# A [1, 576] result accumulated in four column groups of one PSUM bank instead of two groups in two banks

## The chip, the cores and the metric

The kernel runs on one core of one Trainium2 chip. The core has five engines that run side by side and meet through semaphores: TensorE (PE, matrix products), VectorE (DVE), ScalarE (ACT), GpSimd (POOL) and SyncE (SP, here only an issuer of DMAs). Sixteen DMA engines move data between device memory and SBUF, the on-chip memory of 128 partitions. TensorE writes its products into PSUM, which has 128 partitions and eight banks. The metric is the device time of one execution in microseconds; lower is better. The time shown is a median of three runs. A profile is one further execution, and its own time is given beside its span.

A matmul in this kernel computes `lhsT.T @ rhs`: `lhsT` (up to 128 partitions by up to 128 columns) is loaded into the array first, then the columns of `rhs` stream through it. Where `lhsT` has at most 32 columns, only a strip of 32 of the array's columns is needed; the profile calls the loads PEld and the streams PE. `tile_position=(0, 32 * n)` says which of the four strips (column groups 0 to 3) a matmul uses, and its output then lies on the PSUM partitions from 32 n on.

## The reference

One token x of width 576 goes through a layer norm and then through two branches, whose outputs are added to x:

```
xn  = layernorm(x)
A   = attention(xn @ wq, last 4096 keys and values of 16 heads, 32 query heads) @ wo
z   = gelu(xn @ w_in);  z1, z2 = halves of 2304
B   = (z1 * (w_sp * layernorm(z2) + b_sp)) @ w_out
out = x + A + B                          # [1, 1, 576]
```

`wo` is 4096 by 576 and `w_out` 2304 by 576. All inputs and the output are bfloat16. With one token, every product is a vector times a matrix, and almost all of the work is reading: 51 MB of keys, values and weights.

## The kernel before, in words

Everything that is read in bulk goes through one queue, SyncE's, in this order: `wq`, keys of head groups 0 and 1, `w_in`, keys 2, values 0, keys 3, values 1 to 3, `w_out`, `wo`. A head group is four key heads, and there are four groups (index `g`). The buffers are four slots of SBUF (tags a to d) that are reused, so a load waits until its slot was read. `wo` comes in five loads of 14, 9, 6, 2 and 1 "rows" (lines 107 to 109). Such a row is one step of a contraction: 128 partitions by 576 columns. `w_out` has 18 rows (`wout_sb`), `wo` 32 (`wo_sb`).

The order of the instructions on each engine is the order of the program text (the schedule is manual, line 69). For each head group the program turns keys (`keys`, DVE transposes), multiplies them with the queries (`scores`, PE), takes a maximum and an exponential (`sm_a`, DVE and ACT), transposes the probabilities (`sm_b`, DVE and ACT copies, L306), multiplies them with the values (`pv`, L329: eight rounds of four matmuls of 512 columns, one in each column group, into one bank) and normalizes (`tail`: `recip`, `norm`, `y_mms` at L350 and `y_copy` at L357). `y_mms(g)` works in column group g, and `y_copy(g)` puts the 32 values of each partition into `Y`. `Y`, [128, 32], is the attention output, one column for each row of `wo`. The gated branch runs in between: `z_mms` (L365, 162 matmuls with 128 columns of weights and two columns of data), then `z_exp`, `z_gelu` and `z_norm`, which leave `hv`, [128, 18], one column for each row of `w_out`.

The result is accumulated in PSUM in two pieces of 264 and 312 columns (`CUT`), each on one partition: `acc[0]` on partition 0 of one bank, `acc[1]` on partition 32 of another. Line 439 opens both with a product of one and `xrow`, which adds x itself; the first piece reuses the bank from which `zps` has been read. `out_mms` (L465) then adds one row: one column of `hv` or `Y` as weights, 264 columns of data into group 0 and 312 into group 1. All 50 rows are added at the end of the program: after `pv(3)` come the 18 rows of `hv` in three calls of six, with `tail(3)` between the second and the third, then the 32 rows of `Y`, for which the five loads of `wo` are awaited one after the other.

Then the two pieces are copied to `res`, a single row of 576 bfloat16 values: the first by DVE (L480), the second by ACT (L481). ACT issues the store (L482), one run of 1152 bytes.

Around the result the lines are, in the program before:

```python
CUT = (0, 264, D)
        for n in range(2):
            nc.tensor.matmul(acc[n], lhsT=lhs[:, col:col + 1], rhs=wv[:, CUT[n]:CUT[n + 1]],
                             start=False, stop=last, tile_position=(0, 32 * n))
    nc.vector.tensor_copy(res[:, 0:CUT[1]], acc[0])
    nc.scalar.copy(res[:, CUT[1]:D], acc[1])
    nc.scalar.dma_start(out.flatten_outer_dims(), res[:])
```

Of the kernel before, what the change touches and what calls it, by code (L numbers as in the profile page):

```python
# [8 lines left out]
FP32 = mybir.dt.float32  # L9
BF16 = mybir.dt.bfloat16  # L10
# [4 lines left out]
D = 576  # L15
# [10 lines left out]
TC = TP // 2  # L26
NR = 98
NF = FH // 128
CUT = (0, 264, D)
XP = D // 3  # L30
EPS = 1e-5
SCALE = DH ** -0.5
# [5 lines left out]
def kernel(  # L38
# [14 lines left out]
    nc = tc.nc  # L53
    P = nc.NUM_PARTITIONS
# [4 lines left out]
    const = ctx.enter_context(tc.tile_pool(name="const", bufs=1))  # L59
# [4 lines left out]
    ps_o = ctx.enter_context(tc.tile_pool(name="ps_o", bufs=1, space=bass.MemoryType.PSUM))  # L64
    ps_m = ctx.enter_context(tc.tile_pool(name="ps_m", bufs=1, space=bass.MemoryType.PSUM))
    ps_a = ctx.enter_context(tc.tile_pool(name="ps_a", bufs=1, space=bass.MemoryType.PSUM))
    ps_b = ctx.enter_context(tc.tile_pool(name="ps_b", bufs=1, space=bass.MemoryType.PSUM))

    ctx.enter_context(tc.manual_schedule())

# [41 lines left out]
    xrow = const.tile([1, D], BF16, name="xrow")  # L112
# [15 lines left out]
    ones_b = const.tile([1, P], BF16, name="ones_b")  # L128
# [36 lines left out]
    for n in range(2):  # L165
        t = ps_s.tile([P, 2, 512], FP32, name=f"S{n}")
# [15 lines left out]
    for j in range(NS):  # L182
# [8 lines left out]
        out=junk[:], in0=x_col[:], in1=x_col[:], scale=1.0, scalar=0.0,  # L191
# [40 lines left out]
    for k in range(4):  # L232
        for be in range(4):
            nc.tensor.matmul(
                qps2[:, k, be, :].rearrange("p (r g) -> p r g", r=2),
                lhsT=q_rep[0:NR, 2 * k + be // 2, be % 2].rearrange("p a d -> p (a d)"),
                rhs=idq, start=True, stop=True)
# [23 lines left out]
    def scores(g, c):  # L261
        kv = KT.pop((g, c))[:].rearrange("p (t s) b r x e -> p b e x t r s", s=2)
        for be in range(4):
            for x in range(GK):
                nc.tensor.matmul(  # L265
                    S[g % 2][32 * x:32 * x + 8, c, :],
                    lhsT=Qb[:, GK * g + x, be].rearrange("p a h -> p (a h)"),
                    rhs=kv[:, be // 2, be % 2, x],
                    start=(be == 0), stop=(be == 3), tile_position=(0, 32 * x),
                )  # L270
# [161 lines left out]
    zg = z_exp(zps)  # L432
    keys(2, 1)
    scores(2, 1)
    acc = []
    for n, pool in enumerate((ps_a, ps_b)):
        t = pool.tile([P, 512], FP32, name=f"acc{n}", tag="ab"[n])
        acc.append(t[32 * n:32 * n + 1, 0:CUT[n + 1] - CUT[n]])
        nc.tensor.matmul(acc[n], lhsT=ones_b[:, 0:1], rhs=xrow[:, CUT[n]:CUT[n + 1]],
                         start=True, stop=False, tile_position=(0, 32 * n))  # L440
    G, sz = z_gelu(*zg)
    sums(0)
# [18 lines left out]
    pv(3)  # L461

    def out_mms(lhs, col, wv, last):
        for n in range(2):
            nc.tensor.matmul(acc[n], lhsT=lhs[:, col:col + 1], rhs=wv[:, CUT[n]:CUT[n + 1]],  # L465
                             start=False, stop=last, tile_position=(0, 32 * n))

    def out_hv(c):
        for t, wv in wout_sb[6 * c:6 * c + 6]:
            out_mms(hv, t, wv, False)  # L470
# [5 lines left out]
    for t, wv in wo_sb:  # L476
        out_mms(Y, t, wv, t == 31)

    res = const.tile([1, D], BF16, name="res")
    nc.vector.tensor_copy(res[:, 0:CUT[1]], acc[0])  # L480
    nc.scalar.copy(res[:, CUT[1]:D], acc[1])  # L481
    nc.scalar.dma_start(out.flatten_outer_dims(), res[:])  # L482


# [28 lines left out]
```

## Time and profile before

| | |
|---|---|
| median of 3 runs (lowest to highest) | 126.86 us (126.86 to 126.87) |
| profiled execution, its own time | 126.89 us |
| its span, first to last instruction | 125.1 us |
| busy: PE, PEld | 70.8 us (57%), 28.9 us (23%) |
| busy: DVE, ACT, POOL | 78.5 us (63%), 43.2 us (34%), 7.1 us (6%) |
| read from device memory | 50.96 MB, 407 GB/s over the span |
| chain of work that ended last | DMA 61%, DVE 30%, PE 5% |
| mean granted TensorE clock | 0.754 of full speed |

How to read the lines that follow. The page gives the span in 40 equal slices, each digit being a busy share in tenths; PEclk is the TensorE clock that was granted, in tenths of full speed. The chain of waits is followed back from the last instruction and shown in order of time: start, length, what. In the timeline a line is a group of like instructions one after another: start, length, engine, line of the program, operation, tile written <- tiles read, count, and in brackets how long the engine stood idle before and what ended that. In the groups, the numbers behind the bar are busy time in us and the mean length of one in ns, then the idle time before them. "issue" is time in which the engine waited for nothing that the profile shows. Matmuls are pipelined and their ends are modelled; their starts are recorded.

### The profile page before, as it was taken

The page shows a single profiled execution, that of the slowest core. Times are in us where ns is not written, and L with a number is a line of the kernel's source. Part 1 is how long each engine was busy: PE and PEld are TensorE (multiplying, and loading weights), DVE is VectorE, ACT ScalarE, POOL GpSimd, SP SyncE. Part 2 cuts the span into 40 slices and gives each one's busy share as a digit, 9 for nine tenths or more (in the row PEclk, how much of TensorE's full clock was granted, in tenths as well). Part 3 has the DMA queues.
Part 4 walks back from the last instruction along what each step waited for, and adds up shares of the span by engine and source line. Part 5 has one row for each costly group of instructions (what it writes and reads, how often), then busy time and mean ns, then how long its engine had stood idle before and what let it go on. Part 6 is the DMA issues. An engine that isn't in the chain of part 4 may idle for free.

```text
span 125.1 us, 1617 instructions
## 1 busy us (share of the span) xinstructions
PE 70.8 (57%) x626; PEld 28.9 (23%) x626; DVE 78.5 (63%) x150; ACT 43.2 (34%) x101; POOL 7.1 (6%) x19
## 2 busy tenths in 40 slices
PE   0012841009878469998390992059892932049992
PEld 0001201001101013998000131002211411015850
DVE  6745025899799976308999367999938359003301
ACT  2100011000000956996069008707801941940001
POOL 2961000000000000000000000000000100000000
PEclk9999998555995867755559599657998555555899
DMA  4999899998999999898999989999999999999960
GB/s 118 511 422 440 385 471 440 398 492 356 487 420 402 385 493 461 377 492 372 461 451 398 482 367 477 401 451 430 409 482 398 451 394 440 418 413 416 428 237 0
DMA packets 2611, 51.06 MB, mean 408 GB/s; under 512 B 299, under 2 KB 428, under 8 KB 684
## 3 DMA queue, kind: packets, MB, share of 16 engines
q1 hardware_dynamic: 2592, 50.96, 95.2%
q8 instruction: 5, 0.08, 0.2%
q14 instruction: 2, 0.02, 0.0%
q10 hardware_dynamic: 12, 0.00, 0.0%
HBM read 50.96 MB, written 0.00 MB: 407 GB/s over the span
## 4 chain that ended last, share of the span: by engine, by line
DMA 61%; DVE 30%; PE 5%; SPq 1%; issue 1%; ACT 0%; DVEq 0%
DMA k<-in_A_k_cache_dram 37%; DMA end<-in_A_wo_dram 25%; DVE kT L258 22%; DVE pt L303 4%; PE S L265 3%; PE acc L465 1%; SPq L82 1%; DVE mx L286 1%; DVE on L343 1%; DVE om L339 1%; PE yps L350 0%; ACT res L481 0%; DVE rs L320 0%; DVE mt L275 0%; DVE mb L281 0%
## 5 line engine op out<-in xcount | busy, mean ns | idle before, releaser
L265 PE MATMUL S<-kT,Qb 128*8 128x512 bf16 x128 | 32.5, 1148 | 23.3 <-DVE kT L258 22.8
L258 DVE STREAM_TRANSPOSE kT<-k 128x1024 f32<-128x1024 f32 x32 | 36.8, 1207 | 6.5 <-DMA k<-in_A_k_cache_dram 6.5
L292 ACT ACTIVATE pz<-S,nm 32x1024 bf16<-32x1024 f32 x16 | 19.1, 1192 | 33.6 <-DVE nm L289 20.6
L306 ACT COPY PT<-pt 32x128 f32<-32x128 f32 x64 | 19.8, 309 | 17.2 <-DVE pt L303 16.5
L329 PE MATMUL ops<-v,PT 128*32 128x512 bf16 x128 | 11.0, 505 | 6.8 <-ACT PT L306 6.8
L265 PEld LDWEIGHTS <-Qb 128*8 128x8 bf16 x128 | 3.5, 96 | 45.0 <-issue 34.8
L303 DVE STREAM_TRANSPOSE pt<-pz 128x1024 f32<-128x1024 f32 x8 | 9.4, 1210 | 0.8 <-ACT pz L292 0.8
L339 DVE SCALAR_TENSOR_TENSOR om<-ops,rs,dmask 128x512 f32<-128x512 f32 x4 | 3.0, 750 | 10.5 <-PE ops L329 10.3
L365 PEld LDWEIGHTS <-win 128*128 128x128 bf16 x126 | 7.9, 165 | 1.9 <-issue 1.9
L365 PE MATMUL zps<-XT,win 128*128 128x2 bf16 x126 | 8.0, 202 | 0.0
L286 DVE TENSOR_REDUCE mx<-S 128x1 f32<-128x1024 f32 x4 | 4.9, 1214 | 3.9 <-PE S L265 3.9
L329 PEld LDWEIGHTS <-PT 128*32 128x32 bf16 x128 | 3.7, 117 | 11.5 <-ACT PT L306 6.9
L226 ACT CAST q_rep<-qps 128x512 bf16<-128x512 f32 x2 | 1.2, 586 | 14.9 <-DVE q_rep L228 14.9
L404 POOL TENSOR_TENSOR mz<-mz,mhalf 128x1 f32<-128x1 f32 x1 | 0.6, 554 | 85.5 <-DVE mz L403 85.5
L183 PE MATMUL ps_x<-ones_b,xtw 1*128 1x1 bf16 x9 | 0.4, 162 | 8.7 <-DVE xtw L181 8.7
L465 PE MATMUL acc<-end,Y 128*1 128x312 bf16 (+1 forms) x64 | 4.9, 285 | 0.3 <-DMA end<-in_A_wo_dram 0.3
L228 DVE CAST q_rep<-qps 128x512 bf16<-128x512 f32 x2 | 1.4, 692 | 5.1 <-PE qps L217 4.5
L481 ACT CAST res<-acc 1x312 bf16<-1x312 f32 x1 | 0.4, 411 | 11.7 <-PE acc L465 11.7
L350 PE MATMUL yps<-on,sel 128*32 128x32 f32 x32 | 2.0, 210 | 4.1 <-DVE on L343 4.1
L343 DVE TENSOR_REDUCE on<-om 128x128 f32<-128x512 f32 x4 | 4.2, 1042 | 0.1
L480 DVE CAST res<-acc 1x264 bf16<-1x264 f32 x1 | 0.4, 420 | 5.2 <-PE acc L465 5.2
L465 PE MATMUL acc<-end,hv 128*1 128x264 bf16 (+1 forms) x36 | 3.6, 360 | 0.0
(92 smaller groups left out, 56.6 us busy)
## 6 DMA issues: line engine op xcount, KB each, us to landing
k<-in_A_k_cache_dram SPq DMA_DIRECT2D x4, 4096.0 KB
v<-in_A_v_cache_dram SPq DMA_DIRECT2D x4, 4096.0 KB, 26.0
win<-in_B_w_in_dram SPq DMA_DIRECT2D x1, 4032.0 KB, 27.1
wq<-in_A_wq_dram SPq DMA_DIRECT2D x1, 3584.0 KB, 12.8
end<-in_B_w_out_dram SPq DMA_DIRECT2D x1, 2592.0 KB, 22.3
end<-in_A_wo_dram SPq DMA_DIRECT2D x1, 2016.0 KB
end<-in_A_wo_dram SPq DMA_DIRECT2D x1, 1296.0 KB
rest<-in_B_w_in_dram SPq DMA_DIRECT2D x1, 1152.0 KB
```

The lines of the kernel that those rows point to most:

```text
L258: nc.vector.transpose(dst[:, 1024 * n:1024 * (n + 1)], src[:, 1024 * n:1024 * (n + 1)])
L265: nc.tensor.matmul(S[g % 2][32 * x:32 * x + 8, c, :], lhsT=Qb[:, GK * g + x, be].rearrange("p a h -> p (a h)"), rhs=kv[:, be // 2, be % 2, x],
L286: nc.vector.tensor_reduce(out=mx[:, 0:1], in_=s[:], op=ALU.max, axis=mybir.AxisListType.XY)
L292: nc.scalar.activation(pz[lo:hi, :, :, x, :], s[lo:hi].rearrange("p a (t r e) -> p (a t) r e", r=8, e=2), ACT.Exp, bias=nm[lo:hi, 0:1], sc ...
L303: nc.vector.transpose(dst[:, 1024 * n:1024 * (n + 1)], src[:, 1024 * n:1024 * (n + 1)])
L306: nc.scalar.copy(PT4[32 * a:32 * a + 32, :, x, :], pt[32 * x:32 * x + 32, :, 2 * a:2 * a + 2])
L329: nc.tensor.matmul(ops[32 * q:32 * q + 32, :], lhsT=d["PT"][:, t0 // 2:t0 // 2 + 2].rearrange("p t x h e -> p (t x h e)"), rhs=V[g][:, t0: ...
L339: nc.vector.scalar_tensor_tensor(out=om[:].rearrange("p c d -> p (c d)"), in0=ops[:], scalar=d["rs"][:, 0:1], in1=dmask[:].rearrange("p c ...
L343: nc.vector.reduce_sum(on[:], om[:].rearrange("p c d -> p d c"), axis=AXX)
L350: nc.tensor.matmul(yps[32 * g:32 * g + 32, :], lhsT=sel[:, dq, :], rhs=d["on"][:, 32 * dq:32 * dq + 32], start=(dq == 0), stop=(dq == 3), ...
L365: nc.tensor.matmul(zps[:, :, t], lhsT=wt[:, t, :], rhs=XT[:, s, :], start=(s == 0 and t == 0), stop=(s == NS - 1 and t == NF - 1), skip_gr ...
L465: nc.tensor.matmul(acc[n], lhsT=lhs[:, col:col + 1], rhs=wv[:, CUT[n]:CUT[n + 1]], start=False, stop=last, tile_position=(0, 32 * n))
```

## The change

The result is accumulated in four pieces of 144 columns in place of 264 + 312. All four lie in one PSUM bank, in the bank that the first piece used before, on partitions 0, 32, 64 and 96 (column groups 0 to 3). The opening product writes all 32 partitions of each group (32 columns of ones as weights), so that every partition of the block holds something; the 50 rows then add to the first partition of each group only. ACT alone copies the whole block of 128 partitions by 144 columns to `res`, which is now [128, 144]; DVE's copy falls away. The store takes the four partitions 0, 32, 64 and 96 as four rows of 288 bytes. The second pool is removed.

```diff
-CUT = (0, 264, D)
+NQ = 4
+QW = D // NQ
...
-    ps_b = ctx.enter_context(tc.tile_pool(name="ps_b", bufs=1, space=bass.MemoryType.PSUM))
...
-    acc = []
-    for n, pool in enumerate((ps_a, ps_b)):
-        t = pool.tile([P, 512], FP32, name=f"acc{n}", tag="ab"[n])
-        acc.append(t[32 * n:32 * n + 1, 0:CUT[n + 1] - CUT[n]])
-        nc.tensor.matmul(acc[n], lhsT=ones_b[:, 0:1], rhs=xrow[:, CUT[n]:CUT[n + 1]],
+    acc = ps_a.tile([P, 512], FP32, name="acc", tag="a")[:, 0:QW]
+    for n in range(NQ):
+        nc.tensor.matmul(acc[32 * n:32 * n + 32], lhsT=ones_b[:, 0:32], rhs=xrow[:, QW * n:QW * (n + 1)],
                          start=True, stop=False, tile_position=(0, 32 * n))
...
     def out_mms(lhs, col, wv, last):
-        for n in range(2):
-            nc.tensor.matmul(acc[n], lhsT=lhs[:, col:col + 1], rhs=wv[:, CUT[n]:CUT[n + 1]],
+        for n in range(NQ):
+            nc.tensor.matmul(acc[32 * n:32 * n + 1], lhsT=lhs[:, col:col + 1], rhs=wv[:, QW * n:QW * (n + 1)],
                              start=False, stop=last, tile_position=(0, 32 * n))
...
-    res = const.tile([1, D], BF16, name="res")
-    nc.vector.tensor_copy(res[:, 0:CUT[1]], acc[0])
-    nc.scalar.copy(res[:, CUT[1]:D], acc[1])
-    nc.scalar.dma_start(out.flatten_outer_dims(), res[:])
+    res = const.tile([P, QW], BF16, name="res")
+    nc.scalar.copy(res[:], acc)
+    nc.scalar.dma_start(out.rearrange("a b (n c) -> (a b n) c", n=NQ), res[:].rearrange("(n r) c -> n r c", n=NQ)[:, 0, :])
```

## The prediction

> **What bounds the kernel now.** I read the page's busy table and slices first, then the chain of waits, then the end of the timeline, then the groups of instructions that the change resembles.
>
> ```profile
> span 125.1 us, 1617 instructions
> ...
> PEclk9999998555995867755559599657998555555899
> DMA  4999899998999999898999989999999999999960
> ```
>
> The DMA row is the one to see: the 16 DMA engines are nine tenths busy or more almost from the start to the 37th slice (some 119 us). No engine is. The chain of waits, in order of time, ends so:
>
> ```profile
> 90.41 30.86 DMA end<-in_A_wo_dram
> 121.27 0.04 issue
> 121.31 1.39 PE acc L465 x17
> 122.70 0.02 issue
> 122.72 0.41 ACT res L481
> ```
>
> So the end is set by the last weights (wo, five chunks of 14, 9, 6, 2 and 1 rows, one row being one step of the contraction), and behind them a short tail of matmul, copy and store. The timeline of that tail (start, length in us):
>
> ```profile
> 117.30 0.20 DVE L357 CAST Y<-yps 32x32 bf16<-32x32 f32 x1 [0.78 <-PE yps L350]
> ...
> 121.31 1.36 PE L465 MATMUL acc<-end,Y 128*1 128x264 bf16 x18 [0.28 <-DMA end<-in_A_wo_dram]
> ...
> 122.38 0.08 PEld L465 LDWEIGHTS <-Y 128*1 128x1 bf16 x1 [0.17 <-issue]
> 122.69 0.42 DVE L480 CAST res<-acc 1x264 bf16<-1x264 f32 x1 [5.20 <-PE acc L465]
> 122.72 0.41 ACT L481 CAST res<-acc 1x312 bf16<-1x312 f32 x1 [11.73 <-PE acc L465]
> 123.19 0.23 ACTq L482 DMA_DIRECT2D out_dram<-res  x1
> ```
>
> The 18 matmuls look like one burst, but they are three. The trace's landings of the 6-, 2- and 1-row chunks complete at 121.27, 121.97 and 122.34, and matmuls start at 121.31, 122.01 and 122.38, each some 0.04 behind. TensorE has the earlier rows done each time, so only the last row's pair (122.38 to 122.67 by the modelled end) is exposed. Then come the two copies side by side, the store's issue (123.185 to 123.41), its packet at 123.90, its landing at 124.28 and 0.83 us of closing barrier. These groups price the change (count | busy us, mean ns):
>
> ```profile
> L329 PE MATMUL ops<-v,PT 128*32 128x512 bf16 x128 | 11.0, 505 | 6.8 <-ACT PT L306 6.8
> L365 PE MATMUL zps<-XT,win 128*128 128x2 bf16 x126 | 8.0, 202 | 0.0
> L465 PE MATMUL acc<-end,Y 128*1 128x312 bf16 x32 | 4.6, 296 | 0.0
> L465 PE MATMUL acc<-end,Y 128*1 128x264 bf16 x32 | 4.3, 275 | 0.3 <-DMA end<-in_A_wo_dram 0.3
> L226 ACT CAST q_rep<-qps 128x512 bf16<-128x512 f32 x2 | 1.2, 586 | 14.9 <-DVE q_rep L228 14.9
> L234 PE MATMUL qps<-ident,q_rep 98*128 98x8 bf16 x16 | 0.6, 176 | 2.8 <-ACT q_rep L226 2.8
> ```
>
> **The change part by part.**
>
> *The 50 rows, four matmuls of 144 in place of 264 + 312.* At full clock the start times of the 312s are 132 ns apart and those of the 264s 112, each at its own pace: the two column groups run beside each other at 2.4 columns a ns and some 2 ns more. Four groups also run together: the four 512-column matmuls of a probability-times-V round (L329) start within 11 ns and rounds follow at 217 ns, in one PSUM bank, as the result will be now. So a row should take 144/2.4 + 2 = 62 ns instead of 132. This is hidden: from Y's copy (117.50) to the 121.27 landing 23 rows need 3.0 us now and 1.4 then, in 3.8. Without that cover each ns a row grows would count 32 times. Exposed is the last row alone. Matmul lengths rise by 20 ns from 264 to 312 columns (273 to 293 in that row), so 144 lasts 223 and the fourth starts 11 ns after the first: 122.378 + 0.011 + 0.223 = 122.61 against 122.67, **-0.06**. Bounds: -0.07 if all four start together; +0.01 if they start 26 ns apart, as the matmuls of L234 do in one column group.
>
> *The opening matmuls (L439)*, four with 32 columns of ones for two: two more of some 0.22 us at 72.9, beside a maximum on DVE and a saturated DMA; nothing on the path. The bank was already the reused one for the first half, so no wait is new, and the other pool falls away.
>
> *Group 3 is no longer free.* The last head group's y matmuls (L350) use column group 3, which the output rows left empty; now 12 rows precede them there. At half clock (granted from 113.06 to 116.47) these take 12 x 122 ns = 1.5 us from 114.43, over by 115.9, and the y matmuls cannot start before DVE's reduction at 116.57. Nothing, as long as the groups overlap.
>
> *Clock.* Being done sooner, TensorE idles from 115.9 to 116.57; the window that earned the full clock at 116.47 was busy throughout. If the clock stays at half, rows take 122 ns: the 14 rows after Y end 1.7 us later at 119.3, the 9 of the next chunk near 120.4, still ahead of 121.27. Only the last row then pays: by the half-clock lengths (427 for 264, 464 for 312) 144 lasts some 335, +0.11 on the term above.
>
> *Copies.* DVE's goes, and with it nothing (it ended at 123.108, ScalarE's at 123.133). ScalarE copies 128x144 instead of 1x312. Its two casts out of PSUM, 586 ns for 512 columns on 128 partitions and 411 for 312 on one, lie on one line of 0.875 ns a column, so partitions seem free: 411 - 168 x 0.875 = 264, **-0.15**. Bounds: -0.18 (the shortest wide ACTIVATE, 128x36, takes 233), -0.09 (L306's 309 ns for 128 columns, carried to 144). It queues behind nothing: ScalarE is idle for 11.7 us before.
>
> *Store.* Four rows of 288 B from four partitions for one of 1152 B. Issue: 225 ns now; SyncE's 128-row loads take 333 to 432, so 0 to +0.11. Packet: 49 ns now, 20 to 22 for xrow's 384 B, so -0.03. If the rows go to different DMA engines the semaphore waits for the last of four: the ten engines that land the last chunk undelayed spread over 0.43 us (120.43 to 120.86) under load, and hardly without load. I take **+0.03**, near the idle end since nothing else moves by then; both ends are -0.03 and +0.4.
> [...]
>
> **Sum:** 0 (landing) - 0.06 - 0.15 + 0.03 = -0.18 us on the profiled execution's 126.89, so 126.71. That execution is 0.03 above the median of 126.86, so 126.68 beside it. Ends: -0.07 - 0.18 - 0.03 = -0.28, and 0.01 - 0.09 + 0.40 = +0.32. A measurement of this kernel can tell about 0.2%, 0.25 us, from no change: the likeliest gain is below that.
>
> **Rivals.**
>
> *A, TensorE's feed becomes the bound (slower).* The change doubles the pairs of weight load and matmul from 100 to 200. The only long dense run in the trace, the 162 pairs of L365, goes at 62 ns a pair, the same at half and full clock, so not by the array's cycles. If that is what the instruction stream can deliver, the 128 pairs of Y's 32 rows take 7.9 us from 117.55, and the last starts at 125.4 instead of 122.39: +3.0 on the forecast, at least 129.7. It decides from 4.83/128 = 38 ns a pair upward. For it: 62 is what this run shows, and the present tail needs just 60 to 66. Against: L365's loads last 165 ns on strided weights against 96 for L234's 128 contiguous columns, which go at 26 ns a pair for 16 pairs; the load explains the 62. 10%.
> [...]
>
> *B, the store eats the gain.* Four short pieces and four completions cost 0.2 to 0.4 instead of 0.03: 126.86 to 127.06. For it: landing follows the packet by 0.38 us now, and the latest of four decides. Against: no other traffic. 14%.
>
> *C, an instruction fetch falls on a late DMA engine.* The page's five 16 KB instruction packets come about every 256 TensorE instructions (197, 530, 731, 957 and 1222 executed). Four DMA engines land the last chunk at 122.04 to 122.34, some 1.6 us behind the ten undelayed (two more lie between); four such packets came before. The fifth, at 120.63, fell behind all data of its engine. With 204 instructions more it comes near 118 and delays a fifth engine to about 122.0 to 122.5: nothing, or +0.1. Only on an already late engine would it cost about 1 us: 127.7. 5%.
>
> *D, half clock at the end.* -0.18 + 0.11 = -0.07: 126.79. 7%.
>
> **How the numbers follow.** The forecast has 64%: 126.68, of itself 126.58 to 126.85. Two in ten of all lie beyond 126.55 and 127.10: above are A, C and a part of B, below a little more than the best end of the sum, for a landing that shifts by some hundredths. Faster by over 0.2% means under 126.61: the better third of the forecast, 23%. Slower means over 127.11: A, C and the dear end of B with some unforeseen cost, 20%. The rest, 57%, is within.
>
> **What would show it.** The last row's first matmul within 0.1 us of 122.38, four starts within some 15 ns; rows 62 ns apart in each group and longer idle times before 119.2 and 121.3; ScalarE's copy near 264 ns; issue under 0.3 us and 1.1 us from its start to landing. Wrong would make it: pairs spaced 38 ns or more with no wait on wo (A), a landing over 1.3 us after the issue (B), a last landing after 122.5 (C).

## The result: 0.4% slower, nearly all of it behind the last weights

Beside each other, the changed kernel took 127.34 us (median of 6 runs, 127.21 to 127.58) and the kernel before 126.88 (126.86 to 126.99): a ratio of 1.0036, 95% interval 1.0023 to 1.0049. A second comparison gave 127.40 against 126.97, 1.0034 (1.0022 to 1.0047). The forecast was a gain of 0.18 us; the loss is 0.46 in the first comparison and 0.43 in the second.

The profiled execution took 127.21 us, its span is 125.4. The middle of the program is the same; the chain of waits of the changed kernel ends with the same links as before (start, length in us, what):

```profile
91.00 30.88 DMA end<-in_A_wo_dram
121.88 0.04 issue
121.92 0.68 PE acc L463 x12
122.60 0.02 issue
122.63 0.28 ACT res L478
```

The timeline of the tail, the lines that answer to those shown of before:

```profile
116.32 1.05 PE L463 MATMUL acc<-end,Y 128*1 128x144 bf16 x56
119.06 0.73 PE L463 MATMUL acc<-end,Y 128*1 128x144 bf16 x36 [1.69 <-DMA end<-in_A_wo_dram]
119.07 0.58 PEld L463 LDWEIGHTS <-Y 128*1 128x1 bf16 x36 [1.85 <-issue]
121.12 1.45 PE L463 MATMUL acc<-end,Y 128*1 128x144 bf16 x36 [1.33 <-DMA end<-in_A_wo_dram]
...
122.63 0.28 ACT L478 CAST res<-acc 128x144 bf16<-128x144 f32 x1 [12.61 <-PE acc L463]
122.94 0.61 ACTq L479 DMA_DIRECT2D out_dram<-res  x1
```

Three things are to be seen. TensorE got faster as the change intends: the 14 rows of the first `wo` chunk, 56 matmuls, are over in 1.05 us, some 62 ns a row, and TensorE then stands idle for 1.69 and 1.33 us before the next chunks. ScalarE's copy got shorter, 0.28 us for 0.41. And the issue of the store, 0.23 us before, takes 0.61. The groups by shape:

```profile
L463 PE MATMUL acc<-end,Y 128*1 128x144 bf16 x128 | 3.2, 241 | 3.1 <-DMA end<-in_A_wo_dram 3.0
L478 ACT CAST res<-acc 128x144 bf16<-128x144 f32 x1 | 0.3, 278 | 12.6 <-PE acc L463 12.6
```

From the trace's start times and landings, the stretch from the last landing of `wo` to the end of the span, for both profiles of each kernel (us; "before again" and "after again" are second profiles of the same two kernels, see below). The issue is the instruction that hands a DMA to its queue; the landing is the last update of the DMA's semaphore:

| step | before | before again | after | after again |
|---|---|---|---|---|
| last landing of wo, from the span's start | 122.34 | 122.21 | 122.24 | 122.51 |
| landing to the last row's first matmul | 0.04 | 0.04 | 0.04 | 0.04 |
| first matmul to ScalarE's copy | 0.344 | 0.346 | 0.342 | 0.338 |
| ScalarE's copy | 0.411 | 0.409 | 0.278 | 0.279 |
| end of copies to the store's issue | 0.052 | 0.051 | 0.030 | 0.031 |
| start of the issue to the last landing of the result | 1.091 | 1.095 | 1.652 | 1.647 |
| result landed to the end of the span | 0.830 | 0.835 | 0.836 | 0.835 |
| sum from the last landing of wo | 2.77 | 2.78 | 3.18 | 3.17 |

So 0.40 us of the loss lie here: +0.56 at the store, -0.13 at the copy, -0.02 because ScalarE no longer waits for DVE's copy (in both profiles of the kernel before, the issue begins 0.075 to 0.077 us after the end of DVE's copy). The first line scatters by more than the kernels differ in these two pairs; it comes up again under the experiments.

### The profile page after: what moved, and what is told of

It reads as the page before. It is cut to its first block, busy times and chain, and to the rows that moved or that the text cites. A ratio compares the mean times of both kernels' runs of the same rounds, so it can differ in the third digit from the quotient of the medians.

```text
span 125.4 us, 1820 instructions
## 1 busy us (share of the span) xinstructions
PE 67.8 (54%) x728; PEld 27.6 (22%) x728; DVE 78.1 (62%) x149; ACT 43.0 (34%) x101; POOL 7.0 (6%) x19
## 4 chain that ended last, share of the span: by engine, by line
DMA 61%; DVE 30%; PE 4%; SPq 2%; issue 1%; ACT 0%; DVEq 0%
DMA k<-in_A_k_cache_dram 36%; DMA end<-in_A_wo_dram 25%; DVE kT L258 22%; DVE pt L303 4%; PE S L265 3%; SPq L82 2%; DVE mx L286 1%; DVE on L343 1%; DVE om L339 1%; PE acc L463 1%; PE yps L350 0%; DVE rs L320 0%; ACT res L478 0%; DVE mb L281 0%; DVE mt L275 0%
## 5 line engine op out<-in xcount | busy, mean ns | idle before, releaser
L329 PE MATMUL ops<-v,PT 128*32 128x512 bf16 x128 | 10.4, 483 | 6.8 <-ACT PT L306 6.8
L463 PE MATMUL acc<-end,Y 128*1 128x144 bf16 x128 | 3.2, 241 | 3.1 <-DMA end<-in_A_wo_dram 3.0
L245 DVE TENSOR_SCALAR Qb<-qps,mask 128x32 bf16<-128x32 f32 x16 | 2.7, 352 | 1.3 <-PE qps L234 1.3
L163 POOL MEMSET pz<- 128x4096 bf16 x1 | 3.5, 3511 | 0.0
```

Of the source, the lines that this page charges most:

```text
L163: nc.gpsimd.memset(pz[:], 0.0)
L329: nc.tensor.matmul(ops[32 * q:32 * q + 32, :], lhsT=d["PT"][:, t0 // 2:t0 // 2 + 2].rearrange("p t x h e -> p (t x h e)"), rhs=V[g][:, t0: ...
L463: nc.tensor.matmul(acc[32 * n:32 * n + 1], lhsT=lhs[:, col:col + 1], rhs=wv[:, QW * n:QW * (n + 1)], start=False, stop=last, tile_position ...
```

## The experiments

Theory S: the store of four rows costs 0.56 us more than the store of one, and that is the loss. The rivals: M, the doubled matmuls or a later landing; and, on the store itself, P (four partitions), Q (ScalarE's queue), C (first use of the form), and the number of runs. The first four kernels were compared with the kernel before on one chip, where that took 127.00 us.

**Undo the store alone.** Four column groups, but a result on one partition:

```diff
-    res = const.tile([P, QW], BF16, name="res")
-    nc.scalar.copy(res[:], acc)
-    nc.scalar.dma_start(out.rearrange("a b (n c) -> (a b n) c", n=NQ), res[:].rearrange("(n r) c -> n r c", n=NQ)[:, 0, :])
+    res = const.tile([1, D], BF16, name="res")
+    for n in range(NQ):
+        copy = nc.scalar.copy if n % 2 else nc.vector.tensor_copy
+        copy(res[:, QW * n:QW * (n + 1)], acc[32 * n:32 * n + 1])
+    nc.scalar.dma_start(out.flatten_outer_dims(), res[:])
```

> The four column groups of the changed kernel are kept; only its end is undone: four copies of 1x144 (two on DVE, two on ACT) put the pieces side by side on one partition, and the store is one run of 1152 B again. Theory S (the four-row store costs the time: issue 0.607 us against 0.225, landing 1.65 us after the issue's start against 1.09): issue back near 0.23, start to landing near 1.1, and since two copies of some 0.26 in a row replace one of 0.41, 126.8 to 126.95, against 127.34 for the changed kernel. Rival M (the doubled matmuls, or a later landing of wo, cost it): stays at 127.2 to 127.5.

Measured: 127.80 us, 1.0078 (1.0055 to 1.0100). By its time alone neither theory holds. Its timeline says why:

```profile
122.73 0.30 DVE L480 CAST res<-acc 1x144 bf16<-1x144 f32 x1 [6.38 <-PE acc L463]
123.06 0.27 ACT L480 CAST res<-acc 1x144 bf16<-1x144 f32 x1 [12.76 <-DVE res L480]
123.36 0.30 DVE L480 CAST res<-acc 1x144 bf16<-1x144 f32 x1 [0.34 <-ACT res L480]
123.70 0.27 ACT L480 CAST res<-acc 1x144 bf16<-1x144 f32 x1 [0.37 <-DVE res L480]
124.00 0.23 ACTq L481 DMA_DIRECT2D out_dram<-res  x1
```

The four copies, on two engines, wait for each other in turn, 1.24 us in all; the expectation had taken them as two pairs side by side. That each waits for the one before is what the timeline shows; why is not. In the kernel before, the two copies that do run side by side read two different tiles in two banks; here all four read one. The store itself is as S has it: issue 0.228, 1.092 from its start to the landing, as in the kernel before, and not 1.65. The run was made again with two banks, further down.

**The store alone.** Two groups in two banks as before, cut at 288; the result on one partition in four pieces with gaps:

```diff
-CUT = (0, 264, D)
+CUT = (0, 288, D)
+NP = 4
...
-    res = const.tile([1, D], BF16, name="res")
-    nc.vector.tensor_copy(res[:, 0:CUT[1]], acc[0])
-    nc.scalar.copy(res[:, CUT[1]:D], acc[1])
-    nc.scalar.dma_start(out.flatten_outer_dims(), res[:])
+    res = const.tile([1, NP, D // NP + 16], BF16, name="res")
+    half = res[:, 0:NP // 2, 0:D // NP], res[:, NP // 2:NP, 0:D // NP]
+    nc.vector.tensor_copy(half[0], acc[0].rearrange("p (n c) -> p n c", n=NP // 2))
+    nc.scalar.copy(half[1], acc[1].rearrange("p (n c) -> p n c", n=NP // 2))
+    nc.scalar.dma_start(out.rearrange("a b (n c) -> (a b) n c", n=NP), res[:, :, 0:D // NP])
```

> The store alone: two column groups in two banks as in the kernel before (cut at 288 instead of 264, so that it divides by four), the result on one partition in four pieces of 144 with gaps between them, stored as four runs of 288 B. Theory S with the number of runs as the cause: issue 0.55 to 0.65 us, start to landing 1.6, time 127.3 to 127.5. Rival P (what costs is that the rows lie on four partitions): issue near 0.25, time 126.85 to 126.95. Rival M: 126.85 to 126.95 too.

Measured: 127.68 us, 1.0054 (1.0039 to 1.0069). With TensorE's part as in the kernel before, the time is lost all the same. The timeline:

```profile
122.56 0.45 DVE L482 CAST res<-acc 1x288 bf16<-1x288 f32 x1 [5.86 <-PE acc L466]
122.59 0.39 ACT L483 CAST res<-acc 1x288 bf16<-1x288 f32 x1 [12.16 <-PE acc L466]
123.08 0.71 ACTq L484 DMA_DIRECT2D out_dram<-res  x1
```

The issue takes 0.71 us, and 1.75 pass from its start to the last landing. Issue and time are above what S expected (0.55 to 0.65, 127.3 to 127.5): from one partition the four runs cost 0.10 more than from four. So neither the matmuls (M) nor the four partitions (P) are needed for the loss.

**The queue.** The changed kernel with its store issued by SyncE:

```diff
-    nc.scalar.dma_start(out.rearrange("a b (n c) -> (a b n) c", n=NQ), ...
+    nc.sync.dma_start(out.rearrange("a b (n c) -> (a b n) c", n=NQ), ...
```

> The changed kernel with its four-row store issued by SyncE instead of ScalarE. Theory S with the runs as the cause, on any queue: issue 0.5 to 0.65 us, time 127.2 to 127.5. Rival Q (ScalarE's queue is the slow one; SyncE issues 128-row loads in 0.33 to 0.43): issue 0.3 to 0.4, time 127.0 to 127.15.

Measured: 127.40 us, 1.0042 (1.0028 to 1.0056); issue 0.652, 1.650 to the landing. Q falls.

**First use.** The changed kernel with one more DMA of the same form at its start:

```diff
+    early = const.tile([P, QW], BF16, name="early")
+    nc.scalar.dma_start(early[:].rearrange("(n r) c -> n r c", n=NQ)[:, 0, :], A_x.rearrange("a b (n c) -> (a b n) c", n=NQ))
```

> The changed kernel with one more small DMA on ScalarE at the start, of the form of the store (x as four rows of 288 B into four partitions, not used for anything). Theory S with the runs as the cause: the store's issue stays near 0.6 us, time 127.3 to 127.4. Rival C (the form is issued for the first time there, as ScalarE's first load takes 0.50 us to issue and the next two 0.21 and 0.27): the store's issue falls to 0.3 or less, time 126.95 to 127.1.

Measured: 127.54 us, 1.0042 (1.0027 to 1.0057), 0.14 above the expected end, with the last landing of `wo` at 122.56 us in its profile. The instructions on the early tile and on the output (duration in ns, min/median/max):

```profile
L117 ACTq DMA_DIRECT2D early<-in_A_x_dram x1: 604/604/604, 1.8 to 1.8; - x1
...
L481 ACTq DMA_DIRECT2D out_dram<-res x1: 566/566/566, 123.3 to 123.3; - x1
```

The second use takes 0.566 us, only 0.04 less. C falls, as far as a load of this form can stand for the store's first use. And as the first line is a load, the cost does not belong to stores alone.

**Four groups with a one-run store, two banks.** The first experiment repeated so that the copies can run side by side; beside the end as there:

```diff
-    acc = ps_a.tile([P, 512], FP32, name="acc", tag="a")[:, 0:QW]
+    bank = [pool.tile([P, 512], FP32, name="acc", tag="ab"[n])[:, 0:QW] for n, pool in enumerate((ps_a, ps_b))]
...
+    for n in range(NQ):
+        copy = (nc.vector.tensor_copy, nc.scalar.copy)[n // 2]
+        copy(res[:, QW * n:QW * (n + 1)], bank[n // 2][32 * n:32 * n + 1])
```

> The four column groups alone, with groups 0 and 1 in one PSUM bank and 2 and 3 in another, so that DVE copies two pieces while ACT copies the other two (in the run with one bank the four copies went one after the other, DVE, ACT, DVE, ACT). Store one run of 1152 B. Theory S: each engine needs two copies of 0.27 to 0.30 in a row, some 0.55 in place of 0.41, so 126.95 to 127.1 against 127.0 for the kernel before in the last comparison, and the store starts to land as before (issue 0.23, landing 1.1 after it). Rival M (the doubled matmuls cost time): above 127.2 with the last row's copy starting more than 0.45 after its landing.

Measured: 127.23 us against 126.97, 1.0016 (1.0007 to 1.0025). The timeline:

```profile
122.85 0.61 DVE L482 CAST res<-acc 1x144 bf16<-1x144 f32 x2 [5.73 <-PE acc L465]
122.89 0.56 ACT L482 CAST res<-acc 1x144 bf16<-1x144 f32 x2 [12.02 <-PE acc L465]
123.54 0.22 ACTq L483 DMA_DIRECT2D out_dram<-res  x1
```

The store is back at 0.224 and 1.092 us, and from the last landing of `wo` to the end it is 2.92 us: 0.15 more than before, which is the second copy on each engine (0.56 in place of 0.41), less a little at the last row. The time is 0.26 above before, 0.1 more than this stretch explains; the landing is looked at below. At 127.23 us the time is above what S expected and where M had it, but the other half of M's sign is missing: the first copy starts 0.31 after the landing, and not over 0.45. M falls as the main cause, and 0.1 us stay open.

**How the cost grows with the number of runs.** The kernel of the second experiment with `NP = 2` and `NP = 16`.

> Dose: as the run with four pieces from one partition, but two pieces of 576 B. If each further run costs the same (0.225 for one, 0.709 for four, so 0.16 each), the issue takes 0.39; if it is a step between one run and several, 0.6 to 0.7. Start to landing 1.3 or 1.6. Time 127.15 or 127.5.

> Dose: sixteen pieces of 72 B. By 0.16 us for each further run the issue would take 2.6 us and the time be 129.5; if it is a step, 0.6 to 0.8 and 127.5 to 127.7. SyncE's 128-row loads, which issue in 0.33 to 0.43, speak for something between.

Measured: 127.63 us, 1.0045 (1.0029 to 1.0061) for two, and 127.66, 1.0050 (1.0034 to 1.0066) for sixteen. The instructions on the output, two pieces and then sixteen:

```profile
L484 ACTq DMA_DIRECT2D out_dram<-res x1: 707/707/707, 123.3 to 123.3; - x1
```

```profile
L484 ACTq DMA_DIRECT2D out_dram<-res x1: 590/590/590, 123.2 to 123.2; - x1
```

Among these stores it is a step: one run 0.225 us, two 0.707, four 0.709 (0.607 from four partitions), sixteen 0.590. From the issue's start to the last landing it is 1.72 for two and 1.72 for sixteen. Each run beyond the second costs nothing that can be seen.

**A version that might beat before.** The two pieces in two tiles and stored each by its own queue:

```diff
+    nc.sync.dma_start(out.flatten_outer_dims()[:, 0:CUT[1]], res[:])
+    nc.scalar.dma_start(out.flatten_outer_dims()[:, CUT[1]:D], res2[:])
```

> A version that might beat the kernel before: its two pieces in two tiles, each stored by a one-run DMA of its own, DVE's by SyncE and ACT's by ScalarE. Theory: the store no longer waits for the later of the two copies, both issues take 0.23 side by side, so 126.95 to 127.0 against 127.0 for before (a gain of 0.05 at most). If two one-run stores on two queues get in each other's way (issue over 0.3 or landing over 1.2 after it), 127.1 to 127.3.

Measured: 127.24 us, 1.0017 (1.0008 to 1.0027). Slower: SyncE's issue takes 0.323 us, its piece lands 1.275 after the issue's start, and from there it is 0.94 in place of 0.83 to the end. SyncE asks for the semaphores one after another at the end (in the kernel before, these waits begin at 119.22, 121.29, 121.99, 122.35 and 124.29 us), and the last landing belongs to the third of five waits, so two more of some 0.06 us each follow. This is the second expectation's way. No version here beats the kernel before.

**One-run DMAs for the block.** The changed kernel with its four rows stored by four DMAs, two on each queue:

```diff
+    for n in range(NQ):
+        queue = nc.sync if n % 2 else nc.scalar
+        queue.dma_start(out.flatten_outer_dims()[:, QW * n:QW * (n + 1)], res[32 * n:32 * n + 1, :])
```

> The changed kernel, its block copied by ScalarE as one, but the four rows stored by four DMAs of one run each, two on ScalarE's queue and two on SyncE's. Theory S, now that two, four and sixteen runs in one DMA all cost 0.59 to 0.71 us of issue (a step between one run and several): each issue 0.22 to 0.33, the second on a queue ends some 0.55 after the first began, the last landing 1.4 to 1.5 after the first issue in place of 1.65, so 0.15 to 0.25 faster than the changed kernel in the same comparison (127.1 to 127.2). Rival G (the step belongs to stores of 288 B rows or to four completions, not to the DMA's form): last landing 1.6 to 1.9, 127.3 to 127.6.

Measured: 127.69 us, 1.0056 (1.0038 to 1.0073), beside 127.40 for the changed kernel. The instructions on the output:

```profile
L481 SPq DMA_DIRECT2D out_dram<-res x2: 273/296/318, 123.2 to 123.5; - x2
L481 ACTq DMA_DIRECT2D out_dram<-res x2: 225/241/257, 123.2 to 123.4; - x2
```

The expected gain did not come. The form is what was thought: rows of 288 B from four partitions, one run to a DMA, issue in 0.225 to 0.318 us each, so G's first half (the short rows) falls, though landing and time come out where G had them. For they queue up: the last issue begins 0.36 after the first, and the last landing comes 1.60 after the first issue. From there it is 1.07 to the end in place of 0.83, because that landing belongs to the first of SyncE's five closing waits and four more follow (that SyncE issues stores is not the reason: in the run with its four-row store it is 0.84). What the step saves, the second DMA on each queue and these waits use up.

**The changed kernel and the kernel before, profiled again.**

> The changed kernel again, beside the others on one chip. Theory S: the stretch from the last landing of wo to the end of the span is 3.15 to 3.20 us again, wherever that landing falls (122.2 to 122.6 so far), and the time 127.2 to 127.5. If the change also moved the landing, it would fall outside the 122.2 to 122.6 that runs with two groups and with four have shown alike.

> The kernel before, profiled a second time, for the stretch behind the last landing of wo. Theory S: 2.77 us from that landing to the end of the span as in its first profile (3.17 to 3.18 in both profiles of the changed kernel), while the landing itself lies anywhere between 122.2 and 122.7 as in all runs here; time as its own, 126.85 to 127.0. Rival N (the landing is earlier in the kernel before, and part of the loss lies there): landing at 122.3 or earlier and the eleven others' mean of 122.4 stays above it.

Measured: 127.40 us, 1.0034 (1.0022 to 1.0047), and 127.00, 0.9998 (0.9986 to 1.0010). The stretch behind the last landing is 3.17 and 2.78 us, as the table shows. Over all profiles, the landing is at 122.20 to 122.43, 122.31 on average, in the six with two groups, and at 122.24 to 122.68, 122.48 on average, in the eight with four. They overlap, so no single pair tells; the means differ by 0.16, and twice the standard error of that is 0.12. N's own sign is met here (122.21), but the first profile of the same kernel had 122.34, so N is neither shown nor excluded by that alone. One thing does separate them without exception. In all six profiles with two groups the fifth 16 KB instruction packet comes at 120.5 to 121.0 us, at most 0.12 us ahead of the first DMA engine's landing of the last chunk, and four engines land it over 1.3 us behind the first; in all eight with four groups the packet comes at 119.3 to 120.1, which is 0.4 to 1.2 us ahead of that first landing, and five engines are that late. The last landing is then the latest of five and not of four.

**TensorE kept busy.** Ten matmuls into a spare bank in the idle time of the changed kernel; they add nothing to the result:

```diff
         out_mms(Y, t, wv, t == 31)
+        for _ in range({13: 6, 22: 4}.get(t, 0)):
+            nc.tensor.matmul(spare[:], lhsT=ident[:], rhs=wout_sb[0][1][:, 0:512], start=True, stop=True)
```

> The changed kernel with ten matmuls of 512 columns into a spare bank, six after the first chunk of wo and four after the second, where TensorE otherwise waits 1.7 and 1.3 us for data; they add nothing to the result. Theory K (the shorter last row gained nothing because TensorE's idle time let the granted clock fall to half before it): the clock is full at the last row, and from the start of its first matmul to ScalarE's copy it takes 0.30 to 0.31 us, as in the run with two banks, against 0.34 in the changed kernel; time 0.04 below the changed kernel. Rival L (the length of the last matmul does not decide when the copy starts): 0.34 at full clock too.

The stretches before and around the last rows, in the changed kernel and then here (stretch and its length, busy us and instructions, granted clock, DMA share, GB/s):

```profile
117.90:121.33 3.43, 0.94 (x52) 1.00 0.82 327
121.33:123.00 1.67, 1.18 (x36) 0.50 0.08 29
```

```profile
121.33:123.00 1.67, 1.05 (x36) 1.00 0.10 34
```

In the changed kernel TensorE is busy for 0.94 of 3.43 us, and the clock is at half from 121.33 on. Kept busy (without a gap from 117.20 to 121.78 us), it stays at full, and from the last row's first matmul to ScalarE's copy 0.285 us pass in place of 0.342 (the expectation's 0.30 to 0.31 was a little long). K holds, L falls. The run with four DMAs, whose clock halved only at 122.69, after its last row, has 0.285 as well. The time, 127.47 us (1.0056, 1.0016 to 1.0097; one of its five runs took 128.71), doesn't resolve 0.06 us, the more so as the last landing fell at 122.68 here. In the other seven profiles with four groups the full clock ends at 120.28 to 121.33 us in five, ahead of the last row, and at 122.69 and 122.76 in two, just behind it; in the six with two groups it holds past 125 us.

## Why the prediction was wrong

**The step that failed is the store's term:** "I take +0.03, near the idle end since nothing else moves by then; both ends are -0.03 and +0.4." It measured +0.56. Of that, +0.38 is the issue (0.225 to 0.607), +0.15 the time from the end of the issue to the first packet (0.486 to 0.638), +0.03 the rest up to the last of four landings. The sum with the measured term is -0.18 - 0.03 + 0.56 = +0.35. The last row, which gave nothing in place of -0.06, brings it to +0.41, the difference of the two stretches in the table; the rest up to +0.46 is not in that stretch.

The term was bounded by the wrong row. The prediction took SyncE's loads of 333 to 432 ns (L82) for the issue, and of these the shortest: 333 - 225 is its +0.11, while 432 would have made +0.21. The same trace had another family, the eight loads of keys and values (L88), and it was passed over:

```profile
L82 SPq DMA_DIRECT2D end<-in_A_wo_dram x5: 382/425/432, 89.5 to 91.3; - x5
L88 SPq DMA_DIRECT2D k<-in_A_k_cache_dram x4: 534/578/642, 1.6 to 59.1; - x4
L88 SPq DMA_DIRECT2D v<-in_A_v_cache_dram x4: 534/538/596, 44.8 to 75.4; - x4
```

All eight of L88 take 534 ns or more. Both families have 128 rows, so the number of rows could not be the measure, and a form that the program had not used could have been as dear as the dearer family: 642 - 225 is +0.42 for the issue alone. With that in place of +0.11 the upper end of the sum is +0.63 and not +0.32, and the measured +0.46 lies inside.

**Rival B, with 14%, comes nearest: the store eats the gain.** But it costs 0.56 and not 0.2 to 0.4, and for another reason than the one given, four short pieces and four completions. The landings of the four pieces lie within 0.07 us, packets of 288 B take 16 to 18 ns each, and pieces of 576, 288 and 72 B cost the same within 0.03 us from issue to landing. Nearly all of the price (0.53 of 0.56) is paid before the first packet moves. So the size of a piece is not what costs here.

**The copy** came as worked out: 278 ns for a forecast of 264, -0.13 for -0.15. That 128 partitions cost ScalarE hardly more than one is shown: its copies of 1x144, in the two runs that have them, take 270 to 273 ns. The term "DVE's goes, and with it nothing" was -0.02.

**The last row** was put at -0.06 and gave nothing (0.344 to 0.342), because rival D happened too: the clock was at half at the last row in five of the eight profiles with four groups. At full clock the four groups give 0.285, the -0.06 of the prediction. That price, 0.057, is half of D's +0.11: the matmuls of the last row take 277 to 280 ns at half clock and not 335. The prediction had D as an exception at 7%, looking at the idle time between 115.9 and 116.57. It had written down the longer one itself (23 rows in 1.4 us of a cover of 3.8) and counted it as cover only.

**The matmuls** went as said: 62 ns a row in each group, four starts within 10 ns, the y matmuls not held up (they begin at 115.60, as DVE's result arrives). Rival A is refuted: 56 pairs in 1.05 us are some 16 ns a pair, well under the 38 from which it would decide.

**Rival C** happened in the mild form described ("delays a fifth engine to about 122.0 to 122.5: nothing, or +0.1"): five late engines in place of four, every time. The packet came at 119.3 to 120.1 and not near 118. A fifth late engine fits the 0.04 to 0.11 us by which the times of the changed kernel, and of the kernel with two banks, exceed what the stretch behind the landing explains. That it is the cause of this remainder was not tested by itself; it would need a kernel with as many TensorE instructions and no matmul more on the way.

**The range** left the result out by 0.24 us. Its upper end was the good half of a bound whose real upper end had not been looked for.

One reading in the prediction is loose and changes nothing: the DMA row is at eight or nine tenths, not at nine throughout, and so up to the 38th slice (118.8 us).

## What to carry to other kernels

A change at the very end of a kernel is priced by every step up to the last semaphore, the issue of the store among them; there, cutting this contiguous store of one run into four cost 0.56 us, four times what the shorter copy gained. When a DMA's shape changes, look in the trace for issues of every shape and queue and take the dearest (0.642 us here, where the store took 0.607), not the one with the likest number of rows; the stores of two and four runs from one partition, at 0.707 and 0.709, went beyond even that. And TensorE, made faster in front of a wait, was idle longer (busy for 0.94 of 3.43 us): the half clock that followed cost the last row 0.057 us, and that is part of the price.

## What the runs showed of the hardware that was not expected

- **The issue of these small DMAs has a step between one run and several.** On ScalarE's queue: one run 0.224 to 0.228 us (1152 B), 0.225 and 0.257 (288 B); two runs 0.707, four 0.709, sixteen 0.590, four rows on four partitions 0.566 to 0.607, a load of four rows 0.604. On SyncE's: one run 0.273 to 0.323, four rows 0.652. The number of landings was the number of runs each time (1, 2, 4, 16), so whether the runs or the number of completions make the step is not separated. It is no rule for every DMA: SyncE's loads of one family (L82) issue in 0.33 to 0.43 with 128 rows, which was not followed up, and ScalarE's one-run loads at the start of the program take 0.21 to 0.34 in the first profiles of the two kernels, the very first 0.50 and 0.53. From one partition the step from one run to two is 0.48 us, and from two runs to sixteen the issue did not grow.
- **Instruction fetches and late DMA engines.** The four or five 16 KB instruction packets that come while the queue is full match in number the four or five DMA engines that land 1.3 to 2.1 us behind the first, in all fourteen profiles. That the packets make the engines late, and the number of TensorE instructions how many, is the author's guess and not shown: no run changes that number alone by enough for one packet more or less.
- **Half clock cost the last row 0.057 us** (0.342 against 0.285) for 144 columns. After 3.43 us (117.90 to 121.33) in which TensorE was busy for 0.94 us the clock was at half; with TensorE busy without a gap from 117.20 to 121.78 us it stayed at full.
